# The last output chunk goes into a buffer that both paths of a branch share, and is stored behind their join

## The chip, the cores and the metric

The kernel runs on one core of one Trainium2 chip. The metric is the device time of one execution in microseconds. Three runs of the kernel before took 743.79, 743.5 and 745.25 us; their median is 743.79 us.

## The reference

Softcapped attention is followed by a gated feed-forward layer without bias:

```python
scores = cap * tanh((q @ k.T / sqrt(64)) / cap)
attn = exp(scores - max(scores)); attn /= sum(attn) + 1e-9
x = (attn @ v) as (4 * 448) rows of 12 * 64
out = (sigmoid(x @ w_gate) * (x @ w_val)) @ w_out        # 1792 x 768, fp32
```

There are 4 batches, 12 heads, 448 positions, a head size of 64, and 1536 columns between the two layers. `cap` is 30. The three weight matrices arrive as 64-bit floats.

## The kernel before, in words

The program loads `cap` and branches on it (L92). If `cap` is at most 32, every engine runs the bounded attention with the feed-forward layer (the path that runs here); if not, it runs a second, separately written path with a general attention. Both paths are laid out in the program one behind the other, first the bounded one, then the general one, and both end at the same place: the kernel's end block, which the profile lists under L1175. An engine that finishes the bounded path has to jump over the instructions of the general path to get there. No engine waits for another at that jump; the engines meet only in the end block, where SP waits for the last transfer of each of the 8 DMA semaphores in turn, and then all five pass a barrier twice.

Every product is made of three passes on fp32 words split into a high and a low part. Attention goes by pairs of heads, and the feed-forward layer by batches (`moe(b)`), with the attention of the next batch put between its matmuls. For batch b, TensorE makes the 12 chunks of the hidden layer (L955), and then the output in two halves of 384 columns (t = 0 and 1, L1093). The rows of a batch are 448 = 3 x 128 + 64. The full chunks of 128 rows are finished batch by batch. The 64 rows that are left over in each batch are kept, and computed in the last batch as two more chunks of 128 rows: chunk 3 has the rest of batches 0 and 1, chunk 4 that of batches 2 and 3.

The stretch that matters here is the very end, half t = 1 of the last batch (`end` is true). Its five chunks are finished one after the other. Each is copied out of its accumulator by VectorE (L1064) or ScalarE (L1066), times 0.5. Chunks 0 to 2 go into a tile `osb` each and are stored by SP's queue at once (L1069). Chunks 3 and 4 go into one tile `osr`, and after the whole loop four stores of 64 rows leave it (L1112 to L1117): three from SP's queue, and the one of the last batch's rest from ScalarE's queue.

SP issues nearly all transfers of the program. ScalarE's queue issues a transfer in the same order as its computing instructions. The order on TensorE and ScalarE is written out by hand; that on the other engines comes from a scheduler.

`c["pair0"]` is a buffer of 128 x 1536 words that is made ahead of the branch (L65). It holds the first loads, and then the raw weights on their way (L808, L888).

Of the kernel before, what the change touches and what calls it, by code (L numbers as in the profile page):

```python
# [20 lines left out]
P = 128  # L21
# [10 lines left out]
@with_exitstack  # L32
def tile_softcap_attention_then_gated_ffn(
    ctx: ExitStack,
    tc: tile.TileContext,
    q: bass.AP,
    k: bass.AP,
    v: bass.AP,
    cap: bass.AP,
    w_gate: bass.AP,  # L40
    w_val: bass.AP,
    w_out: bass.AP,
    out: bass.AP,
):

    nc = tc.nc
    const = ctx.enter_context(tc.tile_pool(name="const", bufs=1))
    c = {}
    c["ident"] = const.tile([P, P], F32, name="ident")
    make_identity(nc, c["ident"])
    c["ident_r"] = const.tile([P, P], F32R, name="ident_r")
    nc.vector.tensor_copy(c["ident_r"], c["ident"])  # L60
    capv = const.tile([P, 1], F32, name="capv")

    const.tile([P, 24], F32, name="pad_const")
    n0 = 2 * NCH * q.shape[3]
    c["pair0"] = const.tile([P, 3 * n0], F32, name="pair0")  # L65
    c["qk0"] = c["pair0"][:, 0:2 * n0].rearrange("p (i c h d) -> p i c h d", i=2, c=NCH, h=2)
    nc.scalar.dma_start(out=capv, in_=cap.partition_broadcast(P))
    both = (nc.sync, nc.scalar)
    _load_k_packed(nc, both, c["qk0"][:, 1], k, 0, lambda: _load_inside(both, c["qk0"][:, 0], q, 0))
    c["k1"] = c["pair0"][:, 2 * n0:].rearrange("p (c h d) -> p c h d", c=NCH, h=2)  # L70
    _load_k_packed(nc, [nc.sync], c["k1"], k, 1)

    with tc.tile_pool(name="ps_w", bufs=1, space=bass.MemoryType.PSUM) as ps_w:
        ps = ps_w.tile([P, P], F32, name="warm")
        for _ in range(WARM):
            nc.tensor.matmul(ps, c["ident"], c["ident"], start=True, stop=True)

    nc.vector.tensor_scalar(
        capv.bitcast(I32), capv.bitcast(I32), 2 ** 31 - 1, None, ALU.bitwise_and
    )  # L80
    c["cap"] = capv
    bounded = const.tile([1, 1], I32, name="bounded")
    nc.vector.tensor_scalar(bounded, capv[0:1, :], CAP_BOUND, None, ALU.is_le)
    rv = nc.values_load(bounded, min_val=0, max_val=1)
    c["ncap"] = const.tile([P, 1], F32, name="ncap")
    nc.vector.tensor_scalar(c["ncap"], capv, -1.0, None, ALU.mult)
    c["scale"] = const.tile([P, 1], F32, name="scale")
    nc.vector.reciprocal(c["scale"], capv)
    nc.vector.tensor_scalar(c["scale"], c["scale"], 1.0 / math.sqrt(q.shape[3]), None, ALU.mult)

    ins = (q, k, v, w_gate, w_val, w_out, out)
    with tc.If(rv > 0) as branch:  # L92
        _layer(tc, c, _bounded_attention, *ins)
    with branch.Else():
        _layer(tc, c, _general_attention, *ins)


def _pair(src, n):
# [4 lines left out]
def _load_inside(engines, t, src, n):  # L103

    s = _pair(src, n)
    for h in range(2):
        engines[h % len(engines)].dma_start(
            out=t[0:src.shape[2] // NCH, :, h, :],
            in_=s[h].rearrange("(c p) d -> p c d", c=NCH),
        )  # L110
# [623 lines left out]
def _layer(tc, c, attention_of, q, k, v, w_gate, w_val, w_out, out):  # L734
    with ExitStack() as ctx:
        _emit(tc, ctx, c, attention_of, q, k, v, w_gate, w_val, w_out, out)


def _emit(tc, ctx, c, attention_of, q, k, v, w_gate, w_val, w_out, out):
    nc = tc.nc  # L740
    B, H, S, D = q.shape
# [4 lines left out]
    HM = DM // 2  # L746
# [15 lines left out]
    o = _Ops(tc, ctx, c, q, k, v)  # L762
# [165 lines left out]
    R, NR, KR = o.REST, B * o.REST, 3  # L928
    assert NR % P == 0
    g_rest, GR = [], P // R  # L930
# [12 lines left out]
    def next_w(u, converting=True):  # L943
        prepare_w(u, converting)
        store_early(u)
        return w_spl.pop(u)

    def moe(b):
# [13 lines left out]
        rest = []  # L962
        if b == B - 1:
            tiles = []
            for tag, bufs, n in o.rest_tags:
                r = ap.tile([P, n, 2, NR // P, KR, P], F32R, tag=tag, bufs=bufs, name=f"rest{len(tiles)}")
# [55 lines left out]
        if b < B - 1:  # L1022
            if b % GR == 0:
                g_rest.append(dram.tile([P, 2, KF, P], F32R, name=f"grest{b}"))
            nc.sync.dma_start(
                out=g_rest[-1][:, :, :, b % GR * R:(b % GR + 1) * R].bitcast(F32),
                in_=g_spl[:, :, :, rest_cols].bitcast(F32),
            )
        else:
            for x, r in enumerate(rest):  # L1030
                for i in range(2):
                    nc.sync.dma_start(
                        out=r[:, i, b // GR, :, b % GR * R:].bitcast(F32),
                        in_=g_spl[:, i, x * KR:(x + 1) * KR, rest_cols].bitcast(F32),
# [5 lines left out]
        for t in range(2):  # L1040
            acc = []
            for m in range(len(chunks)):
                if m < o.NF:
                    acc.append(ps_m.tile([P, HM], F32, tag="m", name=f"o{b}_{t}_{m}"))
                else:
                    acc.append(o.two_banks(f"o{b}_{t}_{m}")[:, 0, 0:HM])
            dst_t = out[:, t * HM:(t + 1) * HM]
            osr = None
            end = b == B - 1 and t == 1

            def copy_out(m, ps):
                nonlocal osr
                if m == o.NF:
                    tag, bufs = o.out_tag
                    osr = ap.tile([P, NR // P, HM], F32, tag=tag, bufs=bufs, name=f"osr{b}_{t}")
                if m < o.NF:
                    dst = big.tile([P, HM], F32, tag="gate", bufs=3, name=f"osb{b}_{t}_{m}")
                else:
                    dst = osr[:, m - o.NF, :]
                last = end and m == len(acc) - 1  # L1060
                if not last and (m % 2 == 0 and b > 0 or 0 < b < B - 1):

                    with tc.high_priority(offset=2 * AHEAD_OF):
                        nc.vector.tensor_scalar(dst, ps, 0.5, None, ALU.mult)  # L1064
                else:
                    nc.scalar.activation(dst, ps, AF.Copy, scale=0.5)  # L1066
                if m < o.NF:
                    at = b * S + m * P
                    nc.sync.dma_start(out=dst_t[at:at + P], in_=dst)  # L1069

            by_chunk = KF - CLOSE * KU if end else KF
            x = 0
            while x < KF:
                units = []
                if x >= by_chunk:
                    to = KF
                elif 0 < b < B - 1 and x in (0, KF - 2 * KU) or b == t == x == 0:
                    to = x + 2 * KU
                else:
                    to = x + KU  # L1080
                converting = (b, t, to) != (0, 0, KF)
                for y in range(x, to, KU):
                    if y == x or end:
                        units.append((y, next_w(u, converting)))
                    else:
                        units.append((y, w_spl.pop(u)))
                    u += 1
                def product(m, y, w):
                    for kk in range(KU):
                        wh, wl = (w[:, i, kk * HM:(kk + 1) * HM] for i in range(2))  # L1090
                        gh, gl = (chunks[m](i, y + kk) for i in range(2))
                        for i, (a, r) in enumerate(((gh, wl), (gh, wh), (gl, wh))):
                            nc.tensor.matmul(  # L1093
                                acc[m], a, r, start=(y + kk == 0 and i == 0),
                                stop=(y + kk == KF - 1 and i == 2),
                            )

                m = 0
                while m < len(chunks):
                    ms = range(m, m + (2 if m == 0 and 0 < b < B - 1 and to == KF else 1))  # L1100
                    for y, w in units:
                        for mm in ms:
                            product(mm, y, w)
                    for mm in ms:
                        if to == KF:
                            copy_out(mm, acc[mm])
                        yield 3 * (to - x) * HM / S
                    m += len(ms)
                if to > x + KU and not end or not converting:
                    prepare_w(u - 1)  # L1110
                x = to
            if b == B - 1:  # L1112
                ends = dst_t.rearrange("(b s) e -> b s e", s=S)[:, o.FULL:]
                for bb in range(B):
                    m, r = divmod(bb * R, P)
                    queue = nc.scalar if t == 1 and bb == B - 1 else nc.sync
                    queue.dma_start(out=ends[bb], in_=osr[r:r + R, m, :])  # L1117


    MS = {mybir.EngineType.PE, mybir.EngineType.Activation}  # L1120
# [4 lines left out]
    with tc.manual_schedule(engines=MS):  # L1125
# [4 lines left out]
        for b in range(B):  # L1130
            m = moe(b)
# [48 lines left out]
```

## Time and profile before

| | us |
|---|---|
| median of three runs (743.5 to 745.25) | 743.79 |
| the profiled execution, its own time | 743.84 |
| its span, from the first to the last instruction | 742.0 |
| TensorE busy within the span | 732.8 |
| VectorE, ScalarE, GpSimd busy | 487.9, 382.3, 245.2 |

The profiled execution is 1.84 us longer than its span: that part lies outside the instructions of the program. It is 0.05 us from the median of the runs. TensorE is busy through nearly all of the span; the rows below are of the last few microseconds, in which it has nothing to do any more.

### The profile page before, as it was taken

Reading aid. Unit: us, or ns where it says so; the run is one execution under the profiler, and the core shown is the slowest. Engines: PE = TensorE matmul, PEld = TensorE weight load, DVE = VectorE, ACT = ScalarE, POOL = GpSimd, SP = SyncE. Lnnn points to the kernel's source line nnn. Section 1 sums busy time; section 2 is a strip of 40 time slices with the busy share of each in tenths; the row PEclk is TensorE's granted clock in tenths of the full one; section 3 lists DMA queues with packets and bytes.
Section 4 is the critical chain, followed back from the end, with each engine's and each line's share of the span. In section 5 each row is a group of like instructions: output and inputs, shape, how many; then the busy total and the mean of one; then the engine's idle time right before and its main releaser. Section 6 shows DMA issues by size and latency. Waiting matters only on the chain.

```text
span 742.0 us, 10384 instructions
## 1 busy us (share of the span) xinstructions
PE 732.8 (99%) x3885; PEld 638.6 (86%) x3885; DVE 487.9 (66%) x505; ACT 382.3 (52%) x424; POOL 245.2 (33%) x269
## 2 busy tenths in 40 slices
PE   8999999999999999999999999999999999999997
PEld 6556787788788988888899988888899999999996
DVE  3798887887897578988897548889878032322000
ACT  5998675785676666575655156565561011210000
POOL 2364323322432354555436315365563000000000
PEclk9999999999999999999999999999999999999999
DMA  5778797987789964543485954522367847863551
GB/s 126 208 203 225 256 340 252 306 284 232 274 262 367 323 217 139 164 137 117 151 254 172 333 159 142 167 94 100 128 180 250 295 156 226 247 190 104 182 162 58
DMA packets 128595, 151.78 MB, mean 205 GB/s; under 512 B 80920, under 2 KB 107032, under 8 KB 128536
## 3 DMA queue, kind: packets, MB, share of 16 engines
q1 hardware_dynamic: 121384, 144.66, 60.5%
q10 hardware_dynamic: 7152, 6.36, 2.7%
q8 instruction: 33, 0.54, 0.3%
q14 instruction: 26, 0.21, 0.1%
HBM read 118.75 MB, written 31.46 MB: 202 GB/s over the span
## 4 chain that ended last, share of the span: by engine, by line
PE 94%; ACT 3%; DVE 1%; DMA 0%; issue 0%; ACTq 0%; DVEq 0%
PE h L955 47%; PE o L1093 22%; PE sc L416 7%; PE pv L472 7%; PE pv L482 2%; PE pv L481 2%; PE tp L362 1%; PE pv L465 1%; PE tp L250 1%; PE sc L409 1%; PE pv L483 1%; ACT sg L818 1%; PE dn L520 1%; ACT pair L810 1%; ACT rd L501 0%; DMA q<-in_q_dram 0%
## 5 line engine op out<-in xcount | busy, mean ns | idle before, releaser
L955 PE MATMUL h<-xspl,wspl 128*128 128x448 f32 x1728 | 371.4, 370 | 0.0
L955 PEld LDWEIGHTS h<-xspl,wspl 128*128 128x128 f32 x1728 | 321.4, 188 | 36.1 <-issue 10.8
L1093 PE MATMUL o<-wspl,gspl 128*128 128x384 f32 x864 | 157.0, 336 | 0.0
L1093 PEld LDWEIGHTS o<-wspl,gspl 128*128 128x128 f32 x864 | 150.3, 188 | 2.8 <-issue 1.8
L419 ACT ACTIVATE t<-sc,scale 128x896 f32<-128x896 f32 x84 | 80.7, 1003 | 25.0 <-PE sc L416 24.6
L210 DVE TENSOR_TENSOR wspl<-pair,wspl 128x768 fp32r<-128x768 f32 x68 | 75.5, 1111 | 22.5 <-POOL wspl L202 19.4
L202 POOL TENSOR_SCALAR gspl<-gate 128x448 fp32r<-128x448 f32 x48 | 37.9, 790 | 145.6 <-DVE gate L1010 145.6
L424 ACT ACTIVATE t<-t,capv 128x1792 f32<-128x1792 f32 (+1 forms) x48 | 80.4, 1691 | 0.0
L1010 DVE SCALAR_TENSOR_TENSOR gate<-gate,h 128x448 f32<-128x448 f32 x48 | 29.6, 616 | 75.2 <-PE h L955 65.3
L1007 ACT ACTIVATE gate<-h 128x448 f32<-128x448 f32 x48 | 26.0, 542 | 97.3 <-PE h L955 97.0
L528 DVE RECIPROCAL rd<-rd 128x448 f32<-128x448 f32 x24 | 70.8, 2948 | 5.0 <-ACT rd L501 2.6
L416 PE MATMUL sc<-T 64*128 64x448 f32 x486 | 63.9, 389 | 0.3 <-ACT xraw L503 0.2
L204 ACT ACTIVATE wspl<-pair 128x768 fp32r<-128x768 f32 x36 | 30.4, 846 | 64.8 <-PE h L955 63.1
L202 POOL TENSOR_SCALAR wspl<-pair 128x768 fp32r<-128x768 f32 x36 | 33.5, 931 | 84.8 <-PE h L955 34.8
L416 PEld LDWEIGHTS sc<-T 64*128 64x128 f32 x486 | 42.7, 185 | 18.7 <-issue 11.4
L472 PE MATMUL pv<-t,vo 128*128 128x448 f32 x144 | 58.6, 544 | 0.0
L437 POOL TENSOR_TENSOR a<-t 128x448 f32<-128x448 f32 x24 | 31.0, 1291 | 64.7 <-DVE as L210 31.8
L210 DVE TENSOR_TENSOR pl<-t,ph 128x1344 fp32r<-128x1344 f32 x24 | 46.9, 1952 | 8.2 <-ACT ph L204 7.8
L1064 DVE TENSOR_SCALAR osb<-o 128x384 f32<-128x384 f32 x16 | 8.6, 555 | 60.7 <-PE o L1093 60.7
L204 ACT ACTIVATE ph<-t 128x1792 fp32r<-128x1792 f32 x24 | 40.8, 1699 | 14.0 <-PE pv L483 13.9
L472 PEld LDWEIGHTS pv<-t,vo 128*128 128x128 f32 x144 | 26.4, 189 | 22.4 <-issue 18.9
L210 DVE TENSOR_TENSOR gspl<-gate,gspl 128x448 fp32r<-128x448 f32 x48 | 40.6, 847 | 7.1 <-POOL gspl L202 6.9
(95 smaller groups left out, 775.9 us busy)
## 6 DMA issues: line engine op xcount, KB each, us to landing
wspl<-wd SPq DMA_DIRECT2D x72, 768.0 KB, 5.7
wd<-wspl SPq DMA_DIRECT2D x20, 768.0 KB, 5.9
pair<-wr SPq DMA_DIRECT2D x36, 384.0 KB, 3.1
w<-in_moe_w_gate_dram SPq DMA_DIRECT2D x12, 768.0 KB, 6.7
w<-in_moe_w_val_dram SPq DMA_DIRECT2D x12, 768.0 KB, 7.5
w<-in_moe_w_out_dram SPq DMA_DIRECT2D x12, 768.0 KB, 4.8
qk<-in_q_dram SPq DMA_DIRECT2D x44, 112.0 KB, 2.7
wr<-pair SPq DMA_DIRECT2D x12, 384.0 KB, 3.1
```

The costliest lines, as they stand in the source:

```text
L202: self.nc.gpsimd.tensor_scalar(dst, src, 1.0, 1.0, ALU.mult, ALU.mult)
L204: self.nc.scalar.activation(dst, src, AF.Copy)
L210: return e.tensor_sub(dst, src, hi.bitcast(F32))
L416: nc.tensor.matmul(ps[:, j, 0:S], a[rows], r[rows], start=(i == 0), stop=(i == len(ops) - 1))
L419: nc.scalar.activation(Pt[n][:, :, m, :], ps[:, :, 0:S], AF.Tanh, scale=c["scale"])
L424: nc.scalar.activation(t, t, AF.Exp, scale=c["cap"])
L437: nc.gpsimd.tensor_add(a, t[:, 0, :], t[:, 1, :])
L472: nc.tensor.matmul(pvs[n, j], vs[n][:, j * NC + m, :], Pt[n][:, j, m, :], start=False, stop=(m == NF - 1),)
L528: nc.vector.reciprocal(rd, rd)
L955: nc.tensor.matmul(ps, a, r, start=(kk == 0 and i == 0), stop=(kk == KD - 1 and i == 2))
L1010: nc.vector.scalar_tensor_tensor(gate, gate, 1.0, ps, ALU.add, ALU.mult)
L1093: nc.tensor.matmul(acc[m], a, r, start=(y + kk == 0 and i == 0), stop=(y + kk == KF - 1 and i == 2),)
```

## The change

The last chunk (chunk 4 of half t = 1 of the last batch) is copied into the first 384 columns of `c["pair0"]`, in the bounded and in the general path alike. Its store is no longer in either path: one transfer of 128 rows (two groups of 64) from SP's queue stands behind the branch, where both paths join. The two stores of chunk 3 of that half are issued right behind its copy, from ScalarE's queue. The four leftover stores of half t = 0 stay on SP's queue, in the same order.

```diff
@@ entry function @@
     with branch.Else():
         _layer(tc, c, _general_attention, *ins)
+
+    rest = q.shape[2] % P
+    ends = out[:, c["last"].shape[1]:].rearrange("(b s) e -> b s e", s=q.shape[2])
+    nc.sync.dma_start(out=ends[q.shape[0] - P // rest:, q.shape[2] - rest:], in_=c["last"])
@@ moe, copy_out @@
                 last = end and m == len(acc) - 1
+                if last:
+                    dst = c["last"] = c["pair0"][:, 0:HM]
                 if not last and (m % 2 == 0 and b > 0 or 0 < b < B - 1):
...
                 if m < o.NF:
                     at = b * S + m * P
                     nc.sync.dma_start(out=dst_t[at:at + P], in_=dst)
+                elif not last:
+                    ends = dst_t.rearrange("(b s) e -> b s e", s=S)[:, o.FULL:]
+                    for x in range(GR):
+                        (nc.scalar if end else nc.sync).dma_start(
+                            out=ends[(m - o.NF) * GR + x], in_=dst[x * R:(x + 1) * R]
+                        )
@@ moe, behind the loop @@
-            if b == B - 1:
-                ends = dst_t.rearrange("(b s) e -> b s e", s=S)[:, o.FULL:]
-                for bb in range(B):
-                    m, r = divmod(bb * R, P)
-                    queue = nc.scalar if t == 1 and bb == B - 1 else nc.sync
-                    queue.dma_start(out=ends[bb], in_=osr[r:r + R, m, :])
```

What it moves shows on two engines. On SP, at the end of the bounded path before the change (`osb` are the stores of chunks 0 to 2, `osr` those of chunks 3 and 4):

```order
L1069 DMA out_dram<-osb_1_0_6328 128x384
L1069 DMA out_dram<-osb_1_1_6349 128x384
L1069 DMA out_dram<-osb_1_2_6370 128x384
L1117 DMA out_dram<-osr_1_6391 64x384 x3
L92 UNCONDITIONAL_BRANCH
```

And now, with the general path left out at the line of dots (`pair_67` is the shared buffer):

```order
L1075 DMA out_dram<-osb_1_0_6328 128x384
L1075 DMA out_dram<-osb_1_1_6349 128x384
L1075 DMA out_dram<-osb_1_2_6370 128x384
L92 UNCONDITIONAL_BRANCH
...
L99 DMA out_dram<-pair_67 2x64x384
L1181 UNCONDITIONAL_BRANCH
```

SP's jump out of the bounded path stood behind its last store; now it stands behind the store of chunk 2, and the last store comes after the jump. A second branch (L1181) leads from there to the end block, which is the next thing in the program.

On ScalarE, at the same place before the change (`o_1_3` and `o_1_4` are the accumulators of chunks 3 and 4):

```order
L1066 ACTIVATE osr_0_6196<-o_0_3_5998 128x384
L1066 ACTIVATE osb_1_1_6349<-o_1_1_6210 128x384
L1066 ACTIVATE osr_1_6391<-o_1_3_6212 128x384
L1066 ACTIVATE osr_1_6391<-o_1_4_6213 128x384
L1117 DMA out_dram<-osr_1_6391 64x384
L92 UNCONDITIONAL_BRANCH
```

And now:

```order
L1072 ACTIVATE osb_1_1_6349<-o_1_1_6210 128x384
L1072 ACTIVATE osr_1_6391<-o_1_3_6212 128x384
L1079 DMA out_dram<-osr_1_6391 64x384 x2
L1072 ACTIVATE pair_67<-o_1_4_6213 128x384
L92 UNCONDITIONAL_BRANCH
...
L1181 UNCONDITIONAL_BRANCH
```

Two stores now stand between ScalarE's last two copies, and its jump follows the last copy with no store between them. On TensorE, VectorE and GpSimd nothing but the second branch is added, and ahead of these places no instruction of any engine moved.

## Rows read from the trace of the kernel before

**Rows 1.** The page: the span, and busy time by engine.

```profile
span 742.0 us, 10384 instructions
PE 732.8 (99%) x3885; PEld 638.6 (86%) x3885; DVE 487.9 (66%) x505; ACT 382.3 (52%) x424; POOL 245.2 (33%) x269
```

**Rows 2.** Timeline of ScalarE from 724 us: start, length, queue instructions as ACTq.

```profile
727.29 0.49 ACT L1066 ACTIVATE osb<-o 128x384 f32<-128x384 f32 x1 [22.44 <-PE o L1093]
733.48 0.49 ACT L1066 ACTIVATE osr<-o 128x384 f32<-128x384 f32 x1 [5.70 <-PE o L1093]
736.61 0.49 ACT L1066 ACTIVATE osr<-o 128x384 f32<-128x384 f32 x1 [2.63 <-PE o L1093]
737.13 0.57 ACTq L1117 DMA_DIRECT2D out_dram<-osr  x1
```

**Rows 3.** Busy time by stretch: length, engines, then clock, DMA share, GB/s.

```profile
736.50:737.20 0.70, 0.07 (x1) 0.00 (x0) 0.00 (x0) 0.49 (x1) 0.00 (x0) 1.00 0.49 114
737.20:738.20 1.00, 0.00 (x0) 0.00 (x0) 0.00 (x0) 0.00 (x0) 0.00 (x0) 1.00 0.06 16
738.20:739.40 1.20, 0.00 (x0) 0.00 (x0) 0.00 (x0) 0.00 (x0) 0.00 (x0) 0.78 0.63 178
739.40:740.60 1.20, 0.00 (x0) 0.00 (x0) 0.00 (x0) 0.00 (x0) 0.00 (x0) 0.50 0.00 0
740.60:742.00 1.40, 0.00 (x0) 0.00 (x0) 0.00 (x0) 0.00 (x0) 0.00 (x0) 0.50 0.03 12
```

**Rows 4.** Branches of L92, whole span: duration in ns, first and last start.

```profile
L92 ACTq COMPARE_BRANCH  x2: 46/49/52, 4.4 to 737.7; - x2
L92 POOLq COMPARE_BRANCH  x2: 38/42/45, 4.4 to 674.9; - x2
...
L92 DVEq COMPARE_BRANCH  x2: 50/54/57, 4.6 to 730.4; - x2
L92 SPq COMPARE_BRANCH  x2: 46/48/49, 6.5 to 737.6; - x2
```

**Rows 5.** The end block, L1175, from 730 to 741.2 us: instructions by engine.

```profile
L1175 SPq EVENT_SEMAPHORE  x8: 17/28/28, 740.6 to 741.1; - x8
L1175 DVEq DRAIN  x1: 58/58/58, 733.2 to 733.2; - x1
...
L1175 ACTq DRAIN  x1: 80/80/80, 740.7 to 740.7; - x1
```

**Rows 6.** The end block on GpSimd: from 660 us, and from 740.8 us.

```profile
L1175 POOLq DRAIN  x1: 108/108/108, 677.5 to 677.5; - x1
...
L1175 POOLq EVENT_SEMAPHORE  x4: 17/17/17, 741.2 to 741.9; - x4
```

**Rows 7.** The end block on SP from 740.87 us: the fifth wait is its first.

```profile
L1175 SPq EVENT_SEMAPHORE  x6: 17/28/28, 740.9 to 741.9; - x6
L1175 SPq DRAIN  x3: 7/7/13, 741.1 to 741.5; - x3
```

**Rows 8.** Timeline of VectorE from 724 us: its last instruction.

```profile
730.36 0.56 DVE L1064 TENSOR_SCALAR osb<-o 128x384 f32<-128x384 f32 x1 [5.68 <-PE o L1093]
```

**Rows 9.** Leftover stores and ScalarE's waits on L1117, from 724 us.

```profile
L1117 SPq DMA_DIRECT2D out_dram<-osr x3: 467/472/1226, 734.0 to 737.1; - x3
...
L1117 ACTq EVENT_SEMAPHORE  x1: 17/17/17, 736.6 to 736.6; - x1
```

**Rows 10.** Full-chunk stores, L1069, from 724 us, and their landings.

```profile
L1069 SPq DMA_DIRECT2D out_dram<-osb x3: 332/338/338, 724.7 to 730.9; - x3
...
DMA to landing us min/median/max: 1.8/2.0/2.2
```

**Rows 11.** All output stores from 690 us: their landings.

```profile
DMA to landing us min/median/max: 1.8/2.7/4.0
```

**Rows 12.** Pairs of issues on ScalarE's queue: L154, L974, whole span.

```profile
L154 ACTq DMA_DIRECT2D v<-in_v_dram x4: 603/648/1696, 188.4 to 221.6; - x4
...
L974 ACTq DMA_DIRECT2D rest<-grest x12: 499/560/766, 619.5 to 642.6; - x12
```

**Rows 13.** DMA queues from 737 to 740 us: packets, MB, share.

```profile
q8 instruction: 1, 0.02, 2.0%
q14 instruction: 2, 0.02, 1.7%
```

## The prediction

> **What bounds the kernel now.** I read the page first. The span is 742.0 us and TensorE is busy for 732.8 of it [rows 1], so nearly everything is bound by matmuls. The change moves none of them, and no instruction of any engine moves ahead of the last chunks. So only the tail can change: what lies between the last copy and the end of the span.
>
> The timeline of ScalarE dates that copy: it starts at 736.61, lasts 0.49 and ends at 737.10 [rows 2]. The span ends at 742.0. These 4.9 us are the object. The table of stretches shows what fills them [rows 3]: the DMA engines are busy at 0.63 from 738.2 to 739.4, which is the last two stores, and at 0.00 from 739.4 to 740.6. For 1.2 us nothing computes and nothing moves. So the stores are not what the end waits for.
>
> The rows of the branch say what is. SP's jump out of the path is recorded at 737.6 and ScalarE's at 737.7 [rows 4]. The next instruction of either engine, in the end block, is at 740.6 and 740.7 [rows 5]: 3.0 us later on both. VectorE jumps too, at 730.4, and its next instruction is at 733.2, 2.8 us later; GpSimd at 674.9 and 677.5, 2.6 us later [rows 4 to 6]. VectorE and GpSimd had no store out, so the gap belongs to the jump and not to a transfer. Each engine pays it once; for SP and ScalarE it lies behind the last store, where nothing covers it. The transfers of instruction code in this stretch [rows 13] fit that reading.
>
> From 740.6 SP passes its 8 waits, and the barriers follow: 1.4 us to 742.0. The path that sets the end is thus the last copy, SP's issue (at 737.1, about 0.47 long [rows 9]), SP's jump 3.0, the end block 1.4.
>
> [...]
>
> **The change part by part.**
>
> SP's jump. It now stands behind the store of chunk 2, which is issued at 730.9 for 0.33 [rows 10], so SP jumps at about 731.3 and is behind the join at 734.3 by its own 3.0. The last copy ends at 737.1. The jump is covered with 2.8 us to spare, by the matmuls of chunks 3 and 4. If that cover were gone, the 3.0 us would stand ahead of the last store (a rival below).
>
> The last store. SP waits for the copy as before and issues at 737.1. It is now one transfer of 128 rows in place of two of 64 from two queues. The nearest rows are the three stores of 128 rows of the same half, which landed 1.8 to 2.2 us after their issue [rows 10]. I take 2.2, since code is fetched on the same DMA engines while it runs [rows 13], hence 739.3. Below: 1.8, hence 738.9. Above: 4.0, the longest output store from 690 us on [rows 11], hence 741.1.
>
> SP after the landing. The semaphore of the last store is the fifth of its eight waits. In the trace the fifth wait is at 740.9 [rows 7], 1.1 us before the end. By SP, the end is at 739.3 + 1.1 = 740.4.
>
> ScalarE's jump. It no longer waits for a store. A sequencer goes on while its engine still computes: ScalarE's next instruction is recorded at 736.6, when the copy had just begun [rows 9], and VectorE's jump at 730.4, when its last operation (730.36 for 0.56) had just begun [rows 4, 8]. So ScalarE jumps at 736.6 and arrives at 739.6 by its own 3.0. Its drain (0.1) feeds the barrier, which GpSimd collects at 741.2 in the trace, 0.8 before the end [rows 6]. By ScalarE, the end is at 739.6 + 0.1 + 0.8 = 740.5. Bounds: with GpSimd's 2.6 us for a jump it is 740.1; if ScalarE jumps only when its copy is done (737.1), 741.0.
>
> The two stores of chunk 3. On ScalarE they follow the copy that ends at 733.97. The first takes about 0.57 to issue [rows 2]. The second waits its turn: pairs on this queue show 0.5 to 1.7 [rows 12], and the pair on SP 0.47 and 1.23 [rows 9]. They end between 735.1 and 736.3, ahead of the 736.61 at which the last copy can start. Nothing is queued behind them but that copy and the jump. I take nothing, hidden by the matmuls of chunk 4; if the cover failed, each 0.1 us over would be 0.1 us on the end.
>
> The second branch. Each engine's list has one more branch, to the end block that follows directly. The program has such a branch already, the first instruction of each engine, and the trace has no record of it: L92 has two branches per engine, its test and the jump out [rows 4]. I take nothing. Above: 3.0 us, another jump as in the trace, which is a rival.
>
> The stores of half t = 0 are in the same order on the same queue: nothing.
>
> Sum: the end of the span is the later of 740.4 and 740.5, in place of 742.0: 1.5 us less. The profiled execution's own time of 743.84 becomes 742.3; the median of the runs is only 0.05 away from it, so it is 742.3 for the runs too. The case's own bounds: a jump of 2.6 us and an early landing save 1.9 (741.9); a late ScalarE jump saves 1.0 (742.8).
>
> **The rivals.**
>
> The store takes the jump's place. If the last store is slow, its landing is the wait behind the jump that went. A landing after 2.9 us gives 740.0 + 1.1 = 741.1, 0.9 less (742.9); the longest, 4.0, gives 742.2, 0.2 more (744.0). For it: the output stores from 690 us on have a median of 2.7 [rows 11], and code for ScalarE's jump is fetched at the same time. Against it: the three of this size in the same half took 2.2 at most [rows 10].
>
> The second branch stalls like the first. ScalarE jumps at 736.6, arrives at 739.6, jumps again and arrives at 742.6: with 0.1 and 0.8 the end is at 743.5, 1.5 more, or 745.3. It makes the kernel slower from the point at which the second jump takes more than about 1.5 us, since ScalarE has 740.5 against 742.0. For it: it is a branch, and all far jumps in the trace cost 2.6 to 3.0. Against it: the branch at each engine's start left no record.
>
> The jump is not covered. If SP got behind the join only once the last copy is done, the store would start at 737.1 + 3.0 = 740.1, land at 742.3, and the end would be at 743.4: 1.4 more, 745.2. For it: a branch's join could hold the engines together. Against it: the listing has no wait at the jump, and VectorE and GpSimd jumped 7 and 63 us before SP [rows 4].
>
> The jump costs its record alone. The end would then be held by the landing all along, and the change would leave 743.8. For it: the 46 ns of the record. Against it: the DMA engines had been idle for 1.2 us when SP went on [rows 3].
>
> **How the numbers follow.** The forecast (742.3, from 741.9 to 742.8) has 0.74, the slow store 0.13 (742.9 to 744.0), the second stall 0.05, the uncovered jump 0.03, and the jump without a price 0.05. A measurement of this kernel can tell about 0.3% from no change, 2.2 us: below 741.6 is faster, above 746.0 slower. The rows allow a gain of 1.9 at the most, so faster needs the scatter of the runs (743.5 to 745.25) on top of a good case: 0.14. Slower needs a rival at 745.3 and scatter the other way, or something that I don't see: 0.04. No change that can be told: 0.82. The range goes from 741.5, the best case with 0.4 of scatter, to 743.7, which takes in most of the slow stores.
>
> **What would show it.** In the profile after, SP's jump stands at about 731.3 and its next instruction near 734.3, ahead of the last copy; the one store of 128 rows starts at 737.1; ScalarE's drain is near 739.6; no second branch has a record; and the stretch without DMA ahead of the waits is gone. The forecast is wrong if a record of a second branch is followed by microseconds of nothing, if ScalarE's last copy starts later than 736.7, or if the landing comes more than 2.5 us after the issue.

## The result: slower, and the profile after

| | before | after |
|---|---|---|
| median of 6 runs each (us) | 743.88 (743.5 to 745.25) | 748.33 (747.44 to 748.89) |
| ratio after/before, 95% interval | | 1.0057 (1.0047 to 1.0068) |
| profiled execution, its own time and its span | 743.84, 742.0 | 747.44, 745.6 |
| the tail: end of the last copy to end of the span | 4.87 | 8.56 |

The kernel became 4.45 us slower by the medians; 742.3 was forecast. Medians and ratios, here and below, are of fast runs alone: one execution of 1856.05 us (the first kernel with six matmuls, below) and one of 803.91 us (the first with subtractions) are left out. The profiled execution is the quickest of the six after, and again 1.84 us longer than its span, so its tail can be laid beside the tail of before. The bodies agree: the last copy ends at 737.10 before and at 737.08 after. What was lost in this execution was lost behind it, where 8.56 us now stand in place of 4.87.

First the steps that were foreseen. The branch rows of the kernel after, last 146 us (columns as in [rows 4]):

```profile
L92 DVEq COMPARE_BRANCH  x1: 57/57/57, 730.4 to 730.4; - x1
L92 SPq COMPARE_BRANCH  x1: 46/46/46, 731.3 to 731.3; - x1
...
L92 ACTq COMPARE_BRANCH  x1: 43/43/43, 736.6 to 736.6; - x1
```

The instructions of the last store (L99), and those of the end block (now L1181) from 730 to 744.9:

```profile
L99 SPq EVENT_SEMAPHORE  x1: 17/17/17, 733.9 to 733.9; - x1
L99 SPq DMA_DIRECT2D out_dram<-pair x1: 584/584/584, 737.1 to 737.1; - x1
```

```profile
L1181 SPq EVENT_SEMAPHORE  x8: 17/28/28, 737.7 to 744.7; - x8
...
L1181 DVEq DRAIN  x1: 57/57/57, 733.3 to 733.3; - x1
...
L1181 ACTq DRAIN  x1: 75/75/75, 739.2 to 739.2; - x1
```

SP jumps at 731.3 and is behind the join at 733.9, where [rows 4, 5] had the jump at 737.6 and 740.6. ScalarE jumps at 736.6 and arrives at 739.2, VectorE 730.4 and 733.3. The second branch has left no record on any engine. The timeline of ScalarE after answers to [rows 2]:

```profile
733.99 1.92 ACTq L1079 DMA_DIRECT2D out_dram<-osr  x2
736.59 0.49 ACT L1072 ACTIVATE pair<-o 128x384 f32<-128x384 f32 x1 [2.63 <-PE o L1105]
```

The two stores of chunk 3 were issued by 735.9, and the last copy starts at 736.59, as before. So far nothing is late. The stretches of the tail after (columns as in [rows 3]):

```profile
736.50:737.20 0.70, 0.05 (x1) 0.00 (x0) 0.00 (x0) 0.49 (x1) 0.00 (x0) 1.00 0.58 141
737.20:738.30 1.10, 0.00 (x0) 0.00 (x0) 0.00 (x0) 0.00 (x0) 0.00 (x0) 1.00 0.10 22
738.30:743.80 5.50, 0.00 (x0) 0.00 (x0) 0.00 (x0) 0.00 (x0) 0.00 (x0) 0.52 0.12 37
743.80:744.60 0.80, 0.00 (x0) 0.00 (x0) 0.00 (x0) 0.00 (x0) 0.00 (x0) 0.50 0.00 0
744.60:745.64 1.04, 0.00 (x0) 0.00 (x0) 0.00 (x0) 0.00 (x0) 0.00 (x0) 0.50 0.00 0
```

The third line shows the loss. Before, the last 192 KB left in 1.2 us at a DMA share of 0.63. Now the same bytes take 5.5 us at 0.12. A share is a mean over 16 DMA engines, and 0.12 is 2 of 16. The DMA view after, from 738.4 to 743.8:

```profile
DMA packets 128, 0.20 MB, mean 37 GB/s; under 512 B 2, under 2 KB 127, under 8 KB 127
...
q1 hardware_dynamic: 127, 0.19, 11.7%
```

and of the last two stores before, from 738.2 to 739.6:

```profile
DMA packets 162, 0.21 MB, mean 152 GB/s; under 512 B 32, under 2 KB 160, under 8 KB 160
...
q1 hardware_dynamic: 80, 0.10, 29.1%
q10 hardware_dynamic: 80, 0.10, 21.4%
```

The packets under 512 B have 4 bytes each and are read as the writes that close a DMA engine's share. Before there were 32, 16 for each of two stores, and the semaphore of each store was updated 16 times; after there are 2, at 743.19 and 743.77, and the last two updates of the store's semaphore follow at 743.52 and 744.55. The store is issued at 737.10. It lands (the last update of its semaphore) at 744.55, 7.45 us later. The last four of SP's eight closing waits follow right there, and the end comes 1.09 later.

What differs is the form of the store. Each of the last two stores before went to 64 consecutive rows. The one behind the join is written as two groups of 64 rows (`ends[...]` has the shape 2 x 64 x 384), so its outermost dimension is 2. In the trace this store runs on 2 engines (a share of 0.12, and 2 closing writes), each of those two on 16 (16 closing writes). That the outermost dimension of the destination sets this number is not shown by these two profiles alone; the runs with 4 and 8 groups, below, test it. The prediction did not weigh it, and no transfer of the last microseconds before has such a form.

### The profile page after: what moved, and what is told of

Its sections match the earlier page's. It is cut to its first block, busy times and chain, and to the rows that moved or that the text cites. A ratio compares the mean times of both kernels' runs of the same rounds, so it can differ in the third digit from the quotient of the medians.

```text
span 745.6 us, 10382 instructions
## 1 busy us (share of the span) xinstructions
PE 733.0 (98%) x3885; PEld 638.7 (86%) x3885; DVE 488.2 (65%) x505; ACT 382.0 (51%) x424; POOL 243.7 (33%) x269
## 4 chain that ended last, share of the span: by engine, by line
PE 91%; DVE 3%; DMA 2%; ACT 1%; issue 1%; POOL 0%; ACTq 0%; POOLq 0%; DVEq 0%
PE h L959 47%; PE o L1105 21%; PE sc L420 7%; PE pv L476 6%; PE pv L486 2%; PE pv L485 2%; DMA v<-in_v_dram 1%; PE tp L366 1%; PE pv L469 1%; PE tp L254 1%; PE sc L413 1%; DVE rd L532 1%; PE pv L487 1%; PE dn L524 1%; ACT pair L814 0%
## 5 line engine op out<-in xcount | busy, mean ns | idle before, releaser
L206 POOL TENSOR_SCALAR gspl<-gate 128x448 fp32r<-128x448 f32 x48 | 36.4, 759 | 145.6 <-DVE gate L1014 145.6
```

Of the source, the lines that this page charges most:

```text
L206: self.nc.gpsimd.tensor_scalar(dst, src, 1.0, 1.0, ALU.mult, ALU.mult)
```

## The experiments

Theory A: the form of the store, outermost dimension 2, costs the time. Rivals: its place behind the join does; or one queue in place of two does. Once A had been confirmed, a second question was left: with the form mended, why is the gain that was forecast still missing?

**Split in two, same place.** The kernel after, with the store behind the join cut into its two groups:

```diff
-    nc.sync.dma_start(out=ends[q.shape[0] - P // rest:, q.shape[2] - rest:], in_=c["last"])
+    for x in range(P // rest):
+        nc.sync.dma_start(
+            out=ends[q.shape[0] - P // rest + x, q.shape[2] - rest:],
+            in_=c["last"][x * rest:(x + 1) * rest],
+        )
```

> The changed kernel with its one store behind the join split into two stores of 64 rows each, both from SP's queue at the same place. Theory (shape): in the changed kernel the store's packets went one after the other over some 5.1 us because its destination has an outermost dimension of 2, and a transfer is spread over no more DMA engines than that; two stores of 64 rows are spread over all 16. Then the second lands about 3.3 us after the first is issued at 737.1, as the pair on SP at 734.0 did in the kernel before, so at 740.4; the end of the span comes 1.1 later at 741.5, and the time is 743.4. Rival (place): whatever SP issues behind the join is slow, because it follows a jump or because code is fetched beside it; then the time stays at 747 to 749. Rival (one queue): the 128 rows are slow because they come from one queue in place of two; then it stays at 747 to 749 too.

Measured: 744.36 against 744.39 for the kernel before, ratio 0.9998 (0.9989 to 1.0007). The loss is gone, with the same place and the same single queue, but the 743.4 of the expectation is not reached. The timeline of SP, with both issues in one row:

```profile
737.71 2.33 SPq L100 DMA_DIRECT2D out_dram<-pair  x2
```

The second issue took 1.79 of these 2.33 us, and its landing (741.62) is what the end waited for; the tail is 4.97. That landing is 3.9 us behind the first issue; before, with one store from each of two queues, it was 2.8. So the pair from one queue lands about 1.1 us later here, which is far less than the loss. The store's form explains the loss, but the gain does not appear either.

**The form alone, in the old place.** The kernel before, with the last chunk's two stores made one inside the path, ahead of SP's jump:

```diff
-                for bb in range(B):
+                for bb in range(B if t == 0 else B - GR):
...
+                if t == 1:
+                    nc.sync.dma_start(out=ends[B - GR:], in_=osr[:, NR // P - 1, :])
```

> The kernel before, with the two stores of the last chunk replaced by one store of 2 x 64 rows from SP's queue, inside the path and ahead of the jump; nothing else moved. Theory (shape): the store takes the 7.4 us from its issue that it took behind the join, lands at about 744.5, and the end of the span is near 745.6, the time 747.4 to 748.9, though SP's jump stands behind it again and is hidden by it. Rival (place): the store lands like the others some 2.2 to 2.8 us after its issue, and the time is that of the kernel before, 743.9.

Measured: 747.5, ratio 1.0042 (1.0028 to 1.0055). The form alone, without the change, costs most of what the change cost in the medians (3.1 of 4.45 us), and its tail in the profile, 8.52, is that of the kernel after. The timeline of SP, and the end block's waits from 745.6:

```profile
738.38 0.57 SPq L1118 DMA_DIRECT2D out_dram<-osr  x1
```

```profile
L1176 SPq EVENT_SEMAPHORE  x8: 17/28/28, 745.7 to 746.8; - x8
```

From the issue to the landing it is 7.3 us. SP's jump, which ended at 741.9, lies within that and costs nothing here. Neither rival explains the loss.

**One run of 128 rows.** The kernel after, storing to 128 consecutive rows of a scratch tensor:

```diff
-    nc.sync.dma_start(out=ends[q.shape[0] - P // rest:, q.shape[2] - rest:], in_=c["last"])
+    nc.sync.dma_start(out=scratch[:, 384:], in_=c["last"])
```

> The changed kernel with the store behind the join going to 128 consecutive rows of a scratch buffer in place of the output, so that its outermost dimension is 128 on both sides; the last chunk's rows of the output are left out. Same place, same queue, same bytes, same row length and row distance. Theory (shape): packets on all 16 engines, landing 1.8 to 2.4 us after the issue at 737.1, end of the span by ScalarE's jump at 740.0 to 740.5, time 741.8 to 742.4. Rivals (place, one queue): 747 to 749 as in the changed kernel.

Measured: 743.49 against 744.39, ratio 0.9989 (0.998 to 0.9998): 0.8 us less by the ratio and 0.9 by the medians, at the edge of what can be told, where 741.8 to 742.4 was expected. The tail is 4.25, 0.6 less than before. The issue is at 737.05 and the landing at 740.18, 3.1 us later where the prediction took 2.2. The DMA view, first from 737.5 to 738.7, then from 738.7 to 739.8:

```profile
DMA packets 136, 0.20 MB, mean 167 GB/s; under 512 B 15, under 2 KB 135, under 8 KB 135
...
q8 instruction: 1, 0.02, 6.2%
```

```profile
DMA  0000004000003000003000002000101010100090
...
q1 hardware_dynamic: 9, 0.01, 5.2%
```

By 738.7 fifteen of the sixteen closing writes are there. The last nine packets, eight rows and one closing write, come one by one after it: a sixteenth of the store's 144 packets, read as one DMA engine's share, is 1.2 us late. A packet of 16 KB of instruction code (q8) was under way until 738.89, and the late share starts at 738.88.

**Four and eight groups.** To see what lies between 2 and 16, the same scratch store with 4 groups of 32 rows and with 8 of 16 (one execution each):

```diff
...
+    scratch = dram.tile([4, 448, 768], F32, name="scratch")    # or 8
...
+    nc.sync.dma_start(out=scratch[:, 0:P // 4, 384:], in_=c["last"])    # or P // 8
```

> The changed kernel with the store behind the join going to a scratch buffer as 4 groups of 32 rows; the last chunk's rows of the output are left out. Theory (shape: as many DMA engines as the outermost dimension): packets over 2.5 us in place of 5.1, landing 2.5 us earlier than in the changed kernel, 4.9 us after the issue. Rival (any destination in more than one run goes through 2 engines): 5 us of packets as in the changed kernel.

> The same with 8 groups of 16 rows. Theory (shape): packets over 1.3 us and a landing about 3.3 to 3.7 us after the issue. Rival (more than one run goes through 2 engines): 5 us of packets.

The DMA view of the store, 4 groups (738.3 to 741.4) and 8 groups (738.9 to 740.8):

```profile
DMA packets 133, 0.20 MB, mean 66 GB/s; under 512 B 4, under 2 KB 132, under 8 KB 132
```

```profile
DMA packets 137, 0.20 MB, mean 108 GB/s; under 512 B 8, under 2 KB 136, under 8 KB 136
```

4 and 8 closing writes; the packets take 2.8 and 1.6 us, and the landings are 4.5 and 3.2 us after the issue (744.57 and 743.82 us in all). With 2 groups it was 5.45 and 7.45. That is 64, 32 and 16 rows for each DMA engine, at 85, 88 and 100 ns a row. Only powers of two were run.

**The same 64 partitions.** A form that fills the real output with an outermost dimension of 64: VectorE and ScalarE each copy half of the chunk into the same 64 partitions, and one store writes both groups:

```diff
-    nc.sync.dma_start(out=ends[q.shape[0] - P // rest:, q.shape[2] - rest:], in_=c["last"])
+    ends = out[:, c["last"].shape[2]:].rearrange("(b s) e -> s b e", s=q.shape[2])
+    nc.sync.dma_start(out=ends[q.shape[2] - rest:, q.shape[0] - P // rest:], in_=c["last"])
...
+                    two = c["pair0"][0:R, 0:GR * HM].rearrange("p (b e) -> p b e", b=GR)
...
+                        nc.vector.tensor_scalar(two[:, 1], ps[R:2 * R], 0.5, None, ALU.mult)
+                    nc.scalar.activation(two[:, 0], ps[0:R], AF.Copy, scale=0.5)
```

> The changed kernel with the last chunk copied in two halves, by ScalarE rows 0 to 63 and by VectorE rows 64 to 127, into the same 64 partitions of the shared buffer side by side; the one store behind the join then has 64 as its outermost dimension on both sides and writes the same 128 rows of the output. Theory (shape): the transfer is spread over 16 engines; both copies run side by side and end at about 737.15; landing at 739.2 to 739.6, end of the span at 740.3 to 740.7, time 742.1 to 742.6, below both kernels. VectorE's jump moves to 736.6 and arrives at 739.5, no later than ScalarE's. Rivals (place, one queue): 747 to 749.

Measured: 744.15, ratio 0.9994 (0.9985 to 1.0003), where 742.1 to 742.6 was expected. The timeline:

```profile
738.29 0.56 DVE L1069 TENSOR_SCALAR pair<-o 64x384 f32<-64x384 f32 x1 [5.69 <-PE o L1109]
738.88 0.48 ACT L1070 ACTIVATE pair<-o 64x384 f32<-64x384 f32 x1 [3.22 <-DMA out_dram<-osr]
739.39 0.64 SPq L99 DMA_DIRECT2D out_dram<-pair  x1
```

The halves ran one after the other, and that cost 0.6 us ahead of the issue. In the trace ScalarE's copy waits for a semaphore that VectorE's copy raises, though the row names an earlier store. Both read one accumulator tile and write one buffer; which of the two orders them is not shown. The store itself is the quickest last store of the experiments:

```profile
DMA packets 144, 0.20 MB, mean 140 GB/s; under 512 B 16, under 2 KB 144, under 8 KB 144
```

All 16 closing writes and the packets lie within 1.1 us, and it lands 2.7 us after its issue. Here the code packet had ended (740.02) before the store's packets began (740.69), and no share is late. From the start of the first copy to the end of the span it is 4.9 us, in place of 5.4 before.

**A full chunk last, behind the join and in the path.** Half t = 1 is closed in the order of chunks 3, 4, 0, 1, 2, so that the last store is an ordinary one of 128 rows. One kernel has it behind the join, its twin in the path ahead of SP's jump:

```diff
...
-                last = end and m == len(acc) - 1
+                last = end and m == o.NF - 1
...
+                closing = [*range(o.NF, len(chunks)), *range(o.NF)]
...
+                    if end and to == KF:
+                        ms = [closing[m]]
...
+    nc.sync.dma_start(out=out[at:at + P, c["last"].shape[1]:], in_=c["last"])    # not in the twin
```

> The changed kernel with the five chunks of the closing stretch taken in the order 3, 4, 0, 1, 2, so that the last one is a full chunk whose 128 output rows follow one another. Its store stands behind the join as in the changed kernel, but has 128 as its outermost dimension on both sides; the four stores of chunks 3 and 4 are issued earlier, under the matmuls. Theory (shape): like the run with 128 consecutive rows of a scratch buffer, whose tail from the end of the last copy to the end of the span was 4.3 us against 4.9 before: 0.5 to 0.9 us less than the kernel before, 743.4 to 743.9 where that one has 744.4. Rival (place): 747 to 749. Rival (no gain at the join): the tail is 4.9 and the time that of the kernel before.

> The same order of chunks and the same buffer for the last one, but its store stays inside the path, ahead of SP's jump. The two kernels differ in that alone. Theory (the jump costs SP 2.6 to 3.0 us behind the last store where nothing covers it): SP arrives in the end block about 0.4 + 3.0 us after the last copy and passes 8 waits and the barriers in 1.4, so the tail is 4.8 us, that of the kernel before, 0.4 to 0.7 us more than with the store behind the join. Rival (the landing is what counts): the landing takes 3.1 us as in the run with the scratch buffer and both kernels have the same tail of 4.2 to 4.3.

Measured: 743.76 and 743.81 against 743.9 before, ratios 0.9997 (0.9988 to 1.0006) and 0.9996 (0.9987 to 1.0004). The timeline of the first:

```profile
737.17 0.49 ACT L1071 ACTIVATE pair<-o 128x384 f32<-128x384 f32 x1 [2.63 <-PE o L1104]
737.69 0.33 SPq L98 DMA_DIRECT2D out_dram<-pair  x1
```

and of the twin, with its end block on SP:

```profile
737.88 0.49 ACT L1069 ACTIVATE pair<-o 128x384 f32<-128x384 f32 x1 [2.63 <-PE o L1102]
738.39 0.33 SPq L1072 DMA_DIRECT2D out_dram<-pair  x1
```

```profile
L1181 SPq EVENT_SEMAPHORE  x9: 17/28/28, 741.4 to 742.8; - x9
```

The tails are 4.51 and 5.06. In the twin SP is out of its jump at 741.4 and then waits for the landing at 742.28, 3.9 us after the issue. So the jump, though in the old place, hardly sets the end: the landing comes later. Behind the join the landing takes 3.45, again with one late share: fifteen closing writes by 739.26, the last at 740.67. Of the twin's expectation the rival's mechanism holds, that the landing sets the end; but the two tails are not the same, since the landings are not.

**Trying to move the code packet.** If the late share comes from the code packet, moving the packet should mend it. The packet had come 4.1 to 4.5 us after the start of TensorE's branch. First attempt: six small matmuls behind the join, to keep TensorE from its end block, for both twins:

```diff
+        for _ in range(6):
+            nc.tensor.matmul(late, c["ident"], c["ident"], start=True, stop=True)
```

> The kernel with the full chunk last and its store behind the join, and behind the join also six 128 x 128 matmuls on TensorE that wait for the last copy and write a spare accumulator; they keep TensorE from the end block's first instruction for about 1.3 us more. Theory (code packet): in every run so far a 16 KB packet of code started 0.6 to 0.7 us after TensorE's drain in the end block, beside the store's packets, and one part in sixteen of the store landed 1.2 to 2.0 us after the others; with the drain some 1.5 us later that packet comes after the store's, all parts land within 2.2 us of the issue, ScalarE's jump (2.6 us from the start of the copy) is the bound, and the tail from the end of the last copy falls from 4.5 to 3.4 to 3.7 us. Rival (the late part has another cause): the last landing stays 3.1 to 3.5 us after the issue and the tail at 4.2 to 4.5.

> The same six matmuls added to the kernel with the same order of chunks and the store inside the path, ahead of SP's jump. Theory (code packet, and a jump of 2.6 to 3.0 us): the store lands 2.2 us after its issue, but SP arrives in the end block only 0.4 + 2.6 to 3.0 us after the issue and has all its waits before it, so the tail is 4.3 to 4.8 us, about 1 us more than with the store behind the join. Rival (the jump costs little): both tails are the same within 0.3 us.

Measured: 743.48 and 743.46 against 744.43, ratios 0.9991 (0.9982 to 1.0) and 0.9989 (0.998 to 0.9998). Tails 4.18 and 5.21, landings 3.1 and 4.0 us after the issue. The attempt failed: the packet still came at 737.26 in the first, and TensorE's sequencer had reached its closing instruction at 736.5. The expectation's "in every run so far" is also too wide: the same-partition store had no late share, and the first store of the split pair had one of 0.9 us.

```profile
L1187 PEldq DRAIN  x1: 1572/1572/1572, 736.5 to 736.5; - x1
```

Second attempt: one matmul behind the join that needs the result of four subtractions on VectorE, which need the last copy:

```diff
+        nc.vector.tensor_sub(spare, c["last"], c["last"])
+        for _ in range(3):
+            nc.vector.tensor_sub(spare, spare, c["last"])
+        nc.tensor.matmul(late, spare[:, 0:P], c["ident"], start=True, stop=True)
```

> The kernel with the full chunk last and its store behind the join. Behind the join stand also four dependent subtractions of 128 x 384 on VectorE that start from the last copy, and one TensorE matmul that reads their result. The six matmuls of the run before did not hold TensorE's sequencer: its drain was still issued 0.13 us after the last copy, and the 16 KB code packet followed 0.8 us after that. Waiting for VectorE holds the sequencer itself for about 2 us. Theory (code packet): the packet comes 2 us later, after the store's packets; the store lands 2.0 to 2.3 us after its issue, and the tail from the end of the last copy falls to 3.3 to 3.6 us. Time 0.8 to 1.4 us under that of the kernel before. Rival (the late part of the store has another cause): landing at 3.1 to 3.5, tail at 4.2 to 4.5.

> The same operations added to the kernel with the store inside the path, ahead of SP's jump. Theory (code packet, and a jump of 2.6 to 3.0 us): the store lands 2.0 to 2.3 us after its issue, but SP is in the end block only 3.0 to 3.4 us after it: tail 4.4 to 4.8, about 1.1 us more than with the store behind the join. This is the gain that the change was forecast to have, freed from the shape of its store and from the code packet. Rival (the jump costs little): both tails are the same within 0.3 us.

Measured: 743.92 and 743.79 against 744.32, ratios 0.9998 (0.9989 to 1.0007) and 0.9997 (0.9988 to 1.0006); tails 4.18 and 4.51. TensorE was held to 740.0 in the first,

```profile
L1190 PEldq DRAIN  x1: 792/792/792, 740.0 to 740.0; - x1
```

but the packet ran from 737.96 to 739.26, beside the store, as ever. The DMA view from 737.9 to 739.3:

```profile
q1 hardware_dynamic: 136, 0.19, 38.3%
q8 instruction: 1, 0.02, 5.8%
```

The packet doesn't wait for TensorE's last work, so this handle was the wrong one. The traces point at another. In thirteen of the fourteen kernels the packet starts 0.73 to 0.75 us after the record of TensorE's branch ends (1.22 in the other, the first with six matmuls). Here that record runs from 733.64 to 737.20:

```profile
L92 PEldq COMPARE_BRANCH  x1: 3562/3562/3562, 733.6 to 733.6; - x1
```

Both attempts put their work behind that jump, so they left its end, and the packet, where it was. That the packet follows the jump is read from the times; no run moved the jump by itself.

Over the three pairs the store behind the join has the shorter tail each time (by 0.55, 1.03 and 0.33 us, one profiled execution each). In the first two, most of that lies in the landings (3.45 against 3.88 us, 3.13 against 4.03); in the third twin SP is back from its jump at 739.73, just behind the landing at 739.70. In the medians the store behind the join is 0.05 us less, 0.02 more and 0.13 more: no gain that the runs can tell.

## Why the prediction was wrong, point by point

**The last store.** This is the step that failed. It was priced as "one transfer of 128 rows in place of two of 64", by stores of equal size and another form [rows 10], with the longest landing of any output store, 4.0, as the upper end [rows 11]. All of those have an outermost dimension of 64 or 128. This one has 2, runs on 2 of 16 DMA engines and lands after 7.45 us. The 5.25 us over the 2.2 that were taken are all of the miss in the profiled execution: 740.4 + 5.25 = 745.65, and its span is 745.6. The median lies another 0.9 above this execution, within the 1.45 us over which the six runs spread. The kernel split in two (744.36) takes the loss away, and the form alone in the kernel before (747.5) brings it back; that is shown.

**Its smaller part.** Even with 16 DMA engines the last landing of the tail takes 2.7 to 4.0 us, not 2.2. The stores of [rows 10] had hardly any code beside them: the 16 KB packet of that stretch ran from 727.71 to 728.64, and the second store's packets began at 728.65; one of 8 KB ended at 731.89, 0.1 us after the third store's packets began. With the landing of 3.1 that the single run of 128 rows had, the prediction's own sum gives 737.1 + 3.1 + 1.1 = 741.3, 0.7 less than 742.0; measured were 0.8 (ratio 0.9989) and a tail 0.6 shorter. So by the profile about half of the 1.5 forecast was to be had. Whether the times show it is open: the kernel with six matmuls and its store in the path, which has no such gain to take, has the same ratio of 0.9989. In before's trace the last landing is at 739.96, only 0.7 us ahead of SP's return from its jump at 740.64: the next bound stood that close. With that landing the sum gives 739.96 + 1.1 = 741.06, 0.9 less than 742.0. The table of stretches [rows 3] hid this: a DMA share of 0.00 from 739.4 was read as "landed", but the landing is recorded 0.6 us after the last packet there (739.32).

**The rival "the store takes the jump's place"** named the mechanism that decided, with a chance of 0.13, and ended its price at 4.0 us (744.0), which is no end for a form that the trace doesn't hold.

**What held.** SP's jump is covered (731.3 to 733.9; 2.6 us, forecast 3.0). The store is issued at 737.10. After the landing SP takes 1.09 to the end (1.1). ScalarE jumps while it still copies and arrives at 739.2 (739.6). The second branch left no record and no gap. The two stores of chunk 3 delay nothing. "The jump is not covered" and "the second branch stalls" fall by these rows. That the jump costs microseconds without a record stands (its record is 0.05 us on SP and 0.04 on ScalarE, and the next instruction stands 2.6 us later on both); "the jump costs its record alone" falls, though the landing, which it had as the bound before, was only 0.7 us from being it.

**The signs that were named.** The prediction would be wrong "if the landing comes more than 2.5 us after the issue"; that is how it was, with 7.45.

## What to carry to other kernels

For each DMA that a change writes, read the outermost dimension of its destination, and not only the bytes: here two stores merged into one with an outermost dimension of 2 took 7.45 us in place of about 2.8. When a wait is to be removed, find the landing or event right behind it, in the trace's own time stamp: here 3.0 us of jump hid a landing that was only 0.7 us earlier, and that left about 0.9 us to gain. And price an operation only by rows of the same form; if there are none, the upper end of the range is open.

## What the runs showed of the hardware

The 192 KB store's packets took 5.45 us on 2 DMA engines, 2.8 on 4, 1.6 on 8 and 1.1 on 16 (the same-partition form), each row of 1.5 KB taking its engine 85 to 100 ns on 2 to 8. In these four kernels it was 1.2 to 1.3 us from the issue to the first packet; for the store of 128 consecutive rows it was 0.8. From the last packet to the landing of a kernel's last store it was 0.3 to 0.8.

Eight 16-engine stores of the tail had a 16 KB code packet (q8) beside them. In each of them one or two shares came late, and the last of the sixteen landed 1.0 to 2.1 us after the fourteenth. In two such stores that ran when the packet was over, the same-partition one and the second of the split pair, that distance was below 0.05 us. But in the kernel before ScalarE's last store began its packets at 738.62, when the packet was over too (738.48), and its last share still came 0.4 us late; SP's, which began them at 738.25 and so overlapped the packet for 0.2 us, had its last share 0.55 us late. The closing writes of these two shares are the two of this view, from 739.24 to 739.4:

```profile
DMA packets 3, 0.00 MB, mean 10 GB/s; under 512 B 2, under 2 KB 3, under 8 KB 3
```

Two code packets of 8 KB ran beside these (739.02 to 739.47). The stores on 4 and 8 engines overlapped the start of their packets with the 16 KB one for 0.2 and 0.4 us, and no share was more than 0.25 us late. That code packets delay a share is thus argued from the times alone: two attempts to move the large one failed. Its start follows the end of TensorE's branch in the traces, and that is not tested either.
